# A fused attention and feed-forward kernel: the hand-written order of four engines is rearranged in small steps

## The chip, the cores and the metric

The kernel runs on one core of one Trainium2 chip. A core has a matrix engine (TensorE, PE in the profile; PEld is its weight load, which overlaps the products), three engines for elementwise work (VectorE is DVE, ScalarE is ACT, GpSimd is POOL), and a queue engine (SyncE, SP) that only issues transfers. POOL issues transfers too. The metric is the device time of the whole kernel in microseconds (us). Times inside a trace count from the first instruction of the profiled execution.

## The reference

Four batches of eight heads attend over 768 tokens of 64 features. The tokens are cut into 8 blocks of 96. A small network of weights, 8 by 8 for each batch and head, is made nearly doubly stochastic in five rounds, and k and v are mixed across blocks with it. Attention then runs inside each block. The result, 3072 tokens by 512 features, goes through a feed-forward layer with a leaky rectifier:

```
for _ in range(5):
    P = exp(P - max(P, -1)); P = P / (sum(P, -1) + 1e-9); P = P / (sum(P, -2) + 1e-9)
k_sorted = einsum('bhij,bhjcd->bhicd', P, k_b)       # the same for v
scores = (q_b @ k_sorted^T) / sqrt(64)
attn   = softmax(scores);  x = attn @ v_sorted
h = x @ w_in;  g = max(h, 0) + alpha * min(h, 0);  out = g @ w_out
```

w_in is 512 by 2048, w_out is 2048 by 512.

## The kernel before, in words

The program is a graph of 1190 operations, each with an engine or a choice of engines, its reads and its writes. The list `SEQ` at the head of the file fixes the rest by hand: operations are numbered in the order in which they are added, and an engine runs its operations in the order in which `SEQ` names them. A letter behind a number picks the engine where there is a choice (a for ACT, d for DVE, p for POOL; without one the first of the operation's choices). An entry such as `i6Y` is no operation of the graph: it puts six filler products (128x512, on the identity matrix, their result never read) on PE, into the PSUM bank called Y. `arrange` walks the list; `emit` derives the semaphore waits from reads and writes. So each engine is a queue in order: an instruction that waits holds all that stand behind it on its engine.

The work has these stages. A *group* is one block of one batch, 32 in all; groups 0 to 7 are batch 0.

* **The start.** POOL issues the loads of q, k and v of batch 0 (tiles hT, KS0, VST0), then pieces of v of batch 1 (VST1), the four pieces of w_in, k of batch 1 (KS1), half of w_out, and q of batch 1 (QN). DVE and ACT make P doubly stochastic on 32 partitions. PE runs 208 tiny products (L941), fillers (L1047), and the transposes of q of batch 0 in four pieces (L643); ACT empties those into QTz0. P is spread into the mixing matrix BDK (PE L569, DVE L573).
* **k and v of batch 0.** PE mixes k in six units (L630); ACT and DVE empty each into KT0 (L401, "CAST KT" and "ACTIVATE KT"), and a last small copy KT<-KT fills a gap. For v, eight units: a rearranging copy hT<-VST (ACT, DVE or POOL), a mix on PE (L714), a cast into VS0. Most copies go through one helper and so share line L401; their tiles tell them apart.
* **Attention of batch 0**, by group: scores (L759), the negated maximum nm (DVE L765), scores again in the other orientation with the maximum subtracted (L781, L771), exponent into ET (ACT L804), the product with v (L813, psO or psYP), the reciprocal rec (DVE L821), the scale into xq (DVE L826 as one instruction, or ACT L832 as eight), a transpose on PE (L848) and a copy into xT.
* **k and v of batches 1 to 3.** POOL spreads k and v into tiles with zeros (KSz, L655; VDz, L401), PE mixes them (L668 for k, L709 for v), ACT and DVE cast into KT and VS. Batch 1 needs KS1, which POOL's ninth transfer brings. Attention of groups 8 to 31 uses L756 for scores, nf for the maximum, Esb for the exponent, and transposes by DMA, which SP issues (ET<-Esb, xT<-xq, QTz<-QN).
* **Feed-forward.** The first layer (L875, FFN1) works on chunks of 192 tokens (groups 0 and 1, then 2 and 3), then of 384 tokens, into the two banks of psH; ACT takes the negative part (t<-psH, L885) and DVE combines (hT<-t, L889). The second layer (L915, FFN2) runs for each 128 tokens in four quarters of four products into psYP, later also psS; a copy takes it to outstg, and SP stores it.

PE's products for later stages and for the feed-forward are interleaved in one list, so that PE has work while the other engines prepare the next stage.

Of the kernel before, what the change touches and what calls it, by code (L numbers as in the profile page):

```python
# [33 lines left out]
57 i4H 26 58 29 127 59 60 61 62 21 63 126 64 41 65 66 22 85 67 128 68 87 69 83 88 70 13 71 i6Y 72 86 73 74 75  # L34
129 16 76 77 78 134 79 81 80 130 34 82 96 89 12 38 91 90d 94 95 97d 144 92 98 140 100 84 i9Y 20 101 136 103a
102d 104 17 99d 107a 110 93d 106 105d 111 145 112 108a 146 114 109 154 115 113d 147 15 155 116 148 137 120
117d 118 156 139 119 121d 122 35 157 19 132 124 123d 135 i3Y 125 27 133 158 149 159 i4G 150 160d 151 179 161
180 i2H 152 162d 153 181 36 163 182 188 164 165 166 196 189 205 190 197 192 206 183 191 193 198 207 194 209
184 195 199 185d 213 210 208 186 211 214 221 212 233 187 217 222 138 244 218 215 30 216 200 245 167p 223 201
219 232 202d 248 224 230 246 203 220 142 204 247 266 249 267 258 231 237 234 250 259 251 268 235 141 260 168  # L40
225 269 262 131 261 226 238 227d 263 252 236 239 264 241 286 315d 289 276 228 265 242 305 243 240 253 306 229
280 290 270 279 277 271 293 291 278 272d 287 307 294 292 173 275 295 273 308 170 274d 285 281 297 288 282d 314
296 342 174 283 343 309 284 301 298 310 175 316 311d 302 344 317 299 300 312 345 303 320 313d 328 326 304 321
323d 346 329 332 32 347 169p 348d 324 333 254 353 319 330 331 349 334 255 171p 350 367 335 325 318 382 256 392
383 322 351 393 395 384 394 336 31 352d 365 337 366 357 396 385 416 327 397 398 417 419 399 257 338 176 420
418 400 421 355 422 356d 425 358d 423 339 426 424 428 401 340 427 359 446 354 360d 449 429 447 361 450 368
362d 430 408 451 369 448 409 363 455 364d 431 411 458 456 452 459 410 177 386 453 370 387 457 460 439 388d 371
454 389 479 390d 372 461 402 414 403 488 443 415 404d 476 178 489 480 405 412 477 440 512 406 481 490 438 478
432 485 441d 413 482 433 434d 486 469 513 491 483 487 435 442 484 444 436 509 445d 472 462 510 524 463 506
464d 378 511 470 507 465 377 514 471 466d 508 374 521 525 518 380 522 492 523 519 515 375 526 493 520 379 545  # L50
516d 474 381 542 475 527 560 376 546 554 561 543 468 341 555 544 562 547 473 500 548 501d 499 551 494d 563 502
552 498 556 503d 549 553 535 589 557 550 534 391 590 504 577 505 558d 437 580 578 495 579 581 538 625 591 571
407 496d 582 572 583 533 537 528 586 529 584 530d 536 539 626 585 587 540 569 588 592 531 541 622 532 570d 575
631 623 573 624 627 600 574 172 632 576 598 634 599 601 564 635 602 608 565 628 633 603 610 636 637 609 629
566d 497 606 604 638 655 605d 607 517 639 567 640 373 568d 649 641 611 593 650 652 612 594 595d 656 653 651
642 596 657 597d 654 613 661 643 664 662 667 663 665 658 559 666 684 668 659 676 687 685 696 686 688 677 669
689 697 711 682 690 680 670 702 691 678 693 703 698 467 694 679 683d 704 644 695 699 810 645 692 712 722 646d
660 700 705 713 681 731 714 719 732 723 817 717 720 751 724 744 733 721 728 812 671 725 715 672 729 673d 734
766 718 745 730 752 726 767 647 816 742 706 753 727 618 768 707 674 708d 757 716 743d 748 740 758 754 749 759
741 801 750 755 746 630 621 802 763 747 769 735 619 764 760 736 737d 709 789 776 761 765 803 762 790 813 738  # L60
775 783 777 811 784 786 778d 615 836 785 787 791 620 788 779 792 614 780d 837 617 795 793 781 616 796 770 782d
830 838 797 814 798 846 815d 818 799 839 844 800 831 845 804 819 821 820 864 822 771 848 865 772 832 874 849d
847 824 823 875 833 825 710 850 826 827 834d 851 872 648 828 805 852 873 829 883 853 675 866 854 876 855 877d
701 858 806 807d 856 878 867 884 859 879 860 885 773 857 840 898 841 880 835 899 861 774 881 944 882 862 900
863 892 842d 889 868 893 886 890 808 894 945 869 891 870 887d 756 924 895 925 901 912 896 926 897 888 913 871
906 843 909 950 910 902 951 739 907 946 903 914 908 952 927 911 918 904d 921 794 919 915 953 922 920 923 970
809 932 971 935 933 916d 947 936 934 972 937 981 938 928 973 939 941 940 996 942 982 905 943 958 997 961 959
929 948d 983 962 960 998 963 984 930d 964 985 967 999 1022 968 954 1023 965 1042 955 1010 969 1024 956d 1043
966 957 974 987 975 976d 931 978 988 1011 989 979 986 980 1048 949 993 1049 977 990 994 1012 995 991 917 992
1025 1007 1004 1008 1044 1009 1005 1050 1006 1019 1016 1000 1020 1013 1051 1001 1017 1021 1068 1018 1045 1002d  # L70
1033 1014d 1046 1003 1030 1069 1034 1026 1031 1079 1027 1035 1070 1032 1080 1028d 1039 1071 1036 1040 1081
1041 1037 1029 1038 1052 1059 1053 1054d 1082 1060 1055 1061 1056 1083d 1100 1057 1084 1058 1065 1047 1062
1066 1124 1067 1063 1064 1085 1072 1086 1076 1087 1125 1077 1073 1074 1078 1091 1088 1101 1092 1075 1089 1093
1126 1090 1015 1097 1094 1098 1102 1099 1095 1096 1109 1106 1110 1127 1111 1107 1108 1115 1112 1116 1103 1117
1113 1114 1121 1104d 1118 1122 1166 1119 1120 1172 1123 1130 1133 1131 1145 1134 1135 1146 1132 1139 1136 1140
1184 1141 1137 1167 1138 1151 1142 1152 1147 1153 1143 1144 1173 1128d 1157 1129 1154 1105 1158 1148 1159 1155
1156 1163 1149 1168 1150 1164 1165 1160 1185 1161 1174 1162 1186 1169 1187 1170 1175 1188 1189 1178 1171 1176
1179 1177 1180 1181 1182 1183
# [1011 lines left out]
```

## Time and profile before

| | us |
|---|---|
| median of 3 runs | 234.44 (234.3 to 235.16) |
| the profiled execution's own time | 234.22 |
| its span, first to last instruction | 232.5 |
| PE busy | 221.9 (95% of the span) |
| DVE busy | 166.5 (72%) |
| ACT busy | 157.6 (68%) |
| POOL busy | 102.7 (44%) |
| granted TensorE clock | 1.000 |

A row of the timeline gives start, duration, engine, line, operation, tiles and shapes, how many instructions are merged in the row, and in brackets the idle time before it with what ended it. The duration of a merged row reaches to the modelled end of its last instruction; PE's products are pipelined, so the next row may start before that end. In the chain of waits a row gives start, duration and what the time went to. In the table by stretches, each row gives the stretch, its length, the busy time with the count of instructions, the granted clock, the share of the DMA engines and the rate in GB/s.

### The profile page before, as it was taken

The page shows a single profiled execution, that of the slowest core. Times are in us where ns is not written, and L with a number is a line of the kernel's source. Part 1 is how long each engine was busy: PE and PEld are TensorE (multiplying, and loading weights), DVE is VectorE, ACT ScalarE, POOL GpSimd, SP SyncE. Part 2 cuts the span into 40 slices and gives each one's busy share as a digit, 9 for nine tenths or more (in the row PEclk, how much of TensorE's full clock was granted, in tenths as well). Part 3 has the DMA queues.
Part 4 walks back from the last instruction along what each step waited for, and adds up shares of the span by engine and source line. Part 5 has one row for each costly group of instructions (what it writes and reads, how often), then busy time and mean ns, then how long its engine had stood idle before and what let it go on. Part 6 is the DMA issues. An engine that isn't in the chain of part 4 may idle for free.

```text
span 232.5 us, 6278 instructions
## 1 busy us (share of the span) xinstructions
PE 221.9 (95%) x2516; PEld 139.3 (60%) x2543; DVE 166.5 (72%) x342; ACT 157.6 (68%) x435; POOL 102.7 (44%) x149
## 2 busy tenths in 40 slices
PE   3998999999999999999999999999999999999995
PEld 3456588685666656665665666555555555555553
DVE  5659599896898978696688677758677675463540
ACT  4369667889989596757888587686684764642332
POOL 7999239859076995863999932000000000000000
PEclk9999999999999999999999999999999999999999
DMA  5999999996996699999749998678515533200033
GB/s 70 218 209 197 215 205 186 184 192 116 192 183 124 64 123 170 172 193 206 155 104 137 107 110 181 131 178 171 97 34 143 116 57 121 63 0 0 10 128 135
DMA packets 73389, 31.36 MB, mean 135 GB/s; under 512 B 64512, under 2 KB 68368, under 8 KB 73360
## 3 DMA queue, kind: packets, MB, share of 16 engines
q0 software_dynamic: 24816, 13.63, 43.3%
q1 hardware_dynamic: 48544, 17.33, 37.1%
q8 instruction: 20, 0.33, 0.6%
q14 instruction: 9, 0.07, 0.1%
HBM read 27.28 MB, written 6.29 MB: 144 GB/s over the span
## 4 chain that ended last, share of the span: by engine, by line
PE 76%; POOL 11%; DMA 9%; issue 2%; ACT 0%; POOLq 0%
PE psH L875 32%; PE psYP L915 29%; DMA KS<-in_k_dram 9%; PE psS L915 4%; PE psS L756 3%; POOL KSz L655 3%; PE psO L813 3%; PE psYP L709 2%; PE psYP L668 2%; POOL VDz L401 1%; POOL QN L491 1%; POOL w_in_bf L960 1%; PE psO L915 1%; POOL QN L431 1%; PE psO L848 1%
## 5 line engine op out<-in xcount | busy, mean ns | idle before, releaser
L889 DVE SCALAR_TENSOR_TENSOR hT<-t,omaT,psH 128x384 bf16<-128x384 f32 (+1 forms) x140 | 76.7, 565 | 30.2 <-ACT t L885 29.4
L875 PE MATMUL psH<-xT,w_in_bf 128*128 128x384 bf16 (+1 forms) x560 | 96.9, 310 | 0.3 <-DVE hT L889 0.3
L885 ACT ACTIVATE t<-psH 128x384 f32<-128x384 f32 x126 | 60.6, 494 | 42.9 <-PE psH L875 42.3
L915 PE MATMUL psYP<-w_out_bf,hT 128*128 128x512 bf16 x309 | 78.4, 379 | 1.4
L875 PEld LDWEIGHTS psH<-xT,w_in_bf 128*128 128x128 bf16 x560 | 50.1, 98 | 29.2 <-DVE hT L889 2.7
L793 ACT ACTIVATE Esb<-psS,nf 96x96 bf16<-96x96 f32 x192 | 46.2, 344 | 2.1 <-DVE nf L765 2.0
L915 PEld LDWEIGHTS psYP<-w_out_bf,hT 128*128 128x128 bf16 x336 | 30.5, 98 | 28.1
L401 POOL COPY VDz<-VST 64x384 bf16<-64x384 bf16 x40 | 33.9, 848 | 16.4 <-PE psH L875 6.5
L655 POOL COPY KSz<-KS 64x512 bf16<-64x512 bf16 x36 | 22.1, 613 | 16.5 <-DMA KS<-in_k_dram 8.0
L765 DVE TENSOR_REDUCE nf<-psS 96x8 f32<-96x768 f32 x24 | 22.8, 950 | 8.9 <-PE psS L756 8.6
L431 POOL DMA_DIRECT2D QN<-in_q_dram x24 | 19.9, 846 | 0.7 <-POOL QN L491 0.6
L826 DVE TENSOR_TENSOR xq<-psO,rec 96x512 bf16<-96x512 f32 x27 | 18.4, 683 | 0.5
L813 PEld LDWEIGHTS psO<-VS,ET 112*128 112x128 bf16 x248 | 11.1, 98 | 3.4 <-ACT xT L401 0.5
L813 PE MATMUL psO<-VS,ET 112*128 112x65 bf16 x248 | 12.7, 194 | 0.0
L756 PEld LDWEIGHTS psS<-KT,QTz 128*128 128x128 bf16 (+1 forms) x192 | 10.7, 101 | 3.3 <-ACT Esb L793 0.2
L756 PE MATMUL psS<-KT,QTz 128*128 128x96 bf16 (+1 forms) x192 | 12.2, 206 | 0.0
L401 DVE CAST VS<-psYP 112x512 bf16<-112x512 f32 x15 | 10.3, 689 | 2.3 <-PE psYP L709 2.3
L821 DVE RECIPROCAL rec<-psO 96x8 f32<-96x8 f32 x31 | 6.2, 200 | 6.1 <-PE psO L813 5.7
L709 PEld LDWEIGHTS psYP<-BDV,VDz 128*128 128x128 bf16 x192 | 8.3, 98 | 3.3 <-POOL VDz L401 0.4
L401 ACT ACTIVATE outstg<-psYP 128x512 f32<-128x512 f32 x11 | 6.6, 603 | 5.0 <-PE psYP L915 4.9
L915 PE MATMUL psS<-w_out_bf,hT 128*128 128x512 bf16 (+1 forms) x48 | 9.8, 344 | 0.0
L709 PE MATMUL psYP<-BDV,VDz 128*128 128x64 bf16 x192 | 9.5, 193 | 0.1
(139 smaller groups left out, 209.6 us busy)
## 6 DMA issues: line engine op xcount, KB each, us to landing
out_dram<-outstg SPq DMA_DIRECT2D x23, 256.0 KB, 2.6
KS<-in_k_dram POOLq DMA_DIRECT2D x3, 768.0 KB, 9.1
QN<-in_q_dram POOLq DMA_DIRECT2D x24, 96.0 KB, 3.8
w_in_bf<-in_moe_w_in_dram POOLq DMA_DIRECT2D x4, 512.0 KB, 16.7
w_out_bf<-in_moe_w_out_dram POOLq DMA_DIRECT2D x2, 1024.0 KB, 18.5
VST<-in_v_dram POOLq DMA_DIRECT2D x4, 384.0 KB, 10.1
hT<-in_q_dram POOLq DMA_DIRECT2D x1, 768.0 KB, 7.3
VST<-in_v_dram POOLq DMA_DIRECT2D x1, 768.0 KB, 13.1
```

Source lines behind the costliest of these rows:

```text
L401: return e.activation(o, i, ACTF.Copy) if e is nc.scalar else e.tensor_copy(o, i)
L431: G.add(POOL, lambda e, h=h: e.dma_start(AP(QN, h * 128 + (h // 4) * 64, [[6144, 128], [1024, 6], [1, 64]]), AP(q.tensor, b * HB + h * S * ...
L655: G.add(POOL, lambda e, hp=hp: e.tensor_copy(AP(KSz, hp * 64 * 3072 + u % 3 * 1024 + hp * 64, [[3072, 64], [128, 8], [1, 64]]), AP(KS[n], ...
L709: inst = e.matmul(AP(t, off + dd * 64, [[row, 128], [1, 64]]), AP(VDz, (u % VSL * 8 + dd) * 128, [[VSL * 1024, 128], [1, 128]]), AP(BDV, b ...
L756: inst = e.matmul(o, AP(QTz[n], hp * 3072 + h4 * 768 + i * 96, [[6144, 128], [1, w]]), AP(KT[n], (h4 * 8 + i) * bk, [[ld, 128], [64, 2], [ ...
L765: G.add(DVE, lambda e: e.tensor_reduce(AP(nx, 0, [[8, 96], [4, 2], [1, 4]]), AP(psX, 0, [[1024, 96], [512, 2], [96, 4], [1, 96]]), AxisLis ...
L793: inst = e.activation(AP(Esb[me], p * 128, [[1024, 96], [64, 2], [1, 48]]), AP(psX, (p // 4) * 512 + (p % 4) * 96, [[1024, 96], [48, 2], [ ...
L813: inst = e.matmul(AP(psZ, hp * 512 + h4 * 68, [[1024, 128], [1, 65]]), AP(ET[me] if far else ET[m], pos(h4, hp) * 96, [[800, nk], [1, 128] ...
L875: inst = e.matmul(AP(pt, poff + x * n, [[1024, 128], [1, n]]), AP(w_in_bf, kt * DFF + (ft + x) * 128, [[KT_TILES * DFF, 128], [1, 128]]), ...
L885: G.add(ACT, lambda e: e.activation(AP(t1[tb], 0, [[384, 128], [1, k * n]]), AP(pt, poff, [[1024, 128], [1, k * n]]), ACTF.Relu, scale=-1. ...
L889: G.add(DVE, lambda e, x=x: e.scalar_tensor_tensor(out=AP(hT, (ft + x) * RING + tok % RING, [[FT_TILES * RING, 128], [1, n]]), in0=AP(t1[t ...
L915: inst = e.matmul(AP(bank[0], bank[1], [[1024, 128], [1, n]]), AP(hT, ft * RING + tok % RING, [[FT_TILES * RING, 128], [1, 128]]), AP(w_ou ...
```

## The change

Only the list `SEQ` is different. All operations of the graph are the same, with the same reads and writes; 50 of them run on the other of ACT and DVE; the fillers are 18 in five places instead of 29 in seven. Its first line and the corresponding one of the change:

```
-0 18 1 4 2 7 3 8 42 43 25 10 44 5 33 40 45 46 24 11 37 47 6 48 49 14 50 51 39 52 28 53 9 54 23 55 i1P 143 56
+0 2 11 18 10 3 1 4 17 7 8 42 43 39 25 5 44 9 45 40 24 46 i2G 47 6 48 49 14 i4P 50 33 51 52 53 23 54 143 55 56
```

What this moves is seen on the engines. POOL's order is the same in both, row for row. The order of the other four differs from the start to the end, in most places by a few rows. Three places:

**DVE, from the mixing matrix of batch 0 to the maximum of group 0** (KT0: mixed k of batch 0; hT<-VST0: rearranging copies of v; nm0: the maximum of group 0). Before:

```order
L573 TENSOR_TENSOR BDK<-mkh,psYP 128x128
L509 TENSOR_REDUCE mkjV<-identf 128x8
L401 CAST KT0<-psH 128x32x2x8
L401 CAST KT0<-psO 128x32x2x8
L401 COPY hT<-VST0 128x8x48
L489 MEMSET ET1 128x16
L401 CAST KT0<-psYP 128x32x2x8
L401 COPY KT0<-KT0 128x32x16
L401 COPY hT<-VST0 128x8x48
L765 TENSOR_REDUCE nm0<-psS 96x8
```

and with the change:

```order
L573 TENSOR_TENSOR BDK<-mkh,psYP 128x128
L401 CAST KT0<-psH 128x32x2x8
L537 TENSOR_REDUCE mkhM<-mkh 128x8
L401 CAST KT0<-psO 128x32x2x8
L401 COPY hT<-VST0 128x8x48 x2
L765 TENSOR_REDUCE nm0<-psS 96x8
```

The third cast of k and the copy KT0<-KT0 have left DVE; they stand on ACT now, ahead of ACT's first copy of v. ACT's five casts and copies of k stand around its copy of q's last piece, two before it and three behind it (two and one before the change). On PE the last piece of q is transposed right behind the other three now, ahead of the spread of P, with no fillers between.

**DVE, from the first reciprocals to the spread of the later batches** (rec1, xq1: group 1; rec0, xq0: group 0; nm0: here the maximum of group 2). Before:

```order
L821 RECIPROCAL rec1<-psYP 96x8
L821 RECIPROCAL rec0<-psO 96x8
L826 TENSOR_TENSOR xq1<-psYP,rec1 96x512
L765 TENSOR_REDUCE nm0<-psS 96x8
L401 COPY xT<-psYP 128x4x96
L595 TENSOR_TENSOR outstg3<-psYP,mkj 128x192
```

and with the change:

```order
L821 RECIPROCAL rec1<-psYP 96x8
L821 RECIPROCAL rec0<-psO 96x8
L826 TENSOR_TENSOR xq1<-psYP,rec1 96x512
L826 TENSOR_TENSOR xq0<-psO,rec0 96x512
L765 TENSOR_REDUCE nm0<-psS 96x8
L401 COPY xT<-psO 128x4x96
L595 TENSOR_TENSOR outstg3<-psYP,mkj 128x192
```

The scale of group 0, eight instructions of ACT before, is one of DVE, ahead of group 2's maximum; the copies into xT of groups 0 and 1 have changed places between ACT and DVE.

**PE, around the fourth to sixth unit of k of batch 1** (L668; the rows run from the fourth to the sixth). Before:

```order
L668 MATMUL psYP<-BDM,KSz 128x64 x8
L875 MATMUL psH<-xT,w_in_bf 128x192 x8
L781 MATMUL psS<-QTz0,KT0 128x96 x8
L771 MATMUL psS<-identb,nm0 128x96 x8
L848 MATMUL psO<-identb,xq2 128x96 x4
L668 MATMUL psYP<-BDM,KSz 128x64 x8
L875 MATMUL psH<-xT,w_in_bf 128x192 x8
L759 MATMUL psS<-KT0,QTz0 128x96 x6
L759 MATMUL psS<-KT0,QTz0 96x96 x2
L668 MATMUL psYP<-BDM,KSz 128x64 x8
```

and with the change:

```order
L668 MATMUL psYP<-BDM,KSz 128x64 x8
L781 MATMUL psS<-QTz0,KT0 128x96 x8
L771 MATMUL psS<-identb,nm0 128x96 x8
L875 MATMUL psH<-xT,w_in_bf 128x192 x8
L848 MATMUL psO<-identb,xq2 128x96 x4
L668 MATMUL psYP<-BDM,KSz 128x64 x8
L875 MATMUL psH<-xT,w_in_bf 128x192 x8
L759 MATMUL psS<-KT0,QTz0 128x96 x6
L759 MATMUL psS<-KT0,QTz0 96x96 x2
L668 MATMUL psYP<-BDM,KSz 128x64 x8
```

The second half of a group's scores has moved ahead of a unit of FFN1. From the list's start to the fifth unit of k, PE has the same products in both lists, apart from the fillers, only in another order.

More of the change, by code (lines that the diff above doesn't have):

```diff
@@ L38 @@
[L38 to L62, printed above, removed]
@@ L79 @@
+1181 1182 1183
 """.split()
```

64 lines of the change are left out of this document (44 added, 20 removed).

## The prediction

> **What bounds the kernel now.** I read the table by stretches first, then the chain of waits, then POOL's and PE's timelines. The stretches are cut where FFN1 begins (28.36) and where PE leaves its one longer wait of the middle (46.13):
>
> ```profile
> 0.00:28.36 28.36, 22.64 (x624) 1.00 0.99 181
> 28.36:46.13 17.77, 17.03 (x286) 1.00 1.52 192
> 46.13:229.80 183.67, 182.18 (x1614) 1.00 0.72 122
> ```
>
> From 46.13 on PE is idle for 183.67 - 182.18 = 1.49 us in 184, so PE bounds that part, and no order of the same products can win more than 1.49 there. Ahead of it the chain of waits runs through something else:
>
> ```profile
> 11.76 21.10 DMA KS<-in_k_dram
> 32.92 0.61 POOL KSz L655
> ...
> 45.46 0.62 POOL KSz L655
> 46.53 0.66 PE psH L875 x8
> ```
>
> The transfer of batch 1's k is issued at 11.76 and lands at 32.9; POOL then spreads it, and hands over to PE at 46.1. On the two engines this reads:
>
> ```profile
> 32.92 0.61 POOL L655 COPY KSz<-KS 64x512 bf16<-64x512 bf16 x1 [8.04 <-DMA KS<-in_k_dram]
> ...
> 40.20 4.30 POOL L655 COPY KSz<-KS 64x512 bf16<-64x512 bf16 x6
> 44.56 0.84 POOL L401 COPY VDz<-VST 64x384 bf16<-64x384 bf16 x1
> 45.46 0.61 POOL L655 COPY KSz<-KS 64x512 bf16<-64x512 bf16 x1
> ```
>
> ```profile
> 28.36 0.83 PE L875 MATMUL psH<-xT,w_in_bf 128*128 128x192 bf16 x8
> ...
> 38.30 0.40 PE L668 MATMUL psYP<-BDM,KSz 128*128 128x64 bf16 x8
> ...
> 46.13 0.41 PE L668 MATMUL psYP<-BDM,KSz 128*128 128x64 bf16 x8 [0.36 <-POOL KSz L655]
> ```
>
> POOL sat idle for 8.04 us until the transfer landed, then worked with hardly a gap; its last copy of k ends at 45.46 + 0.61 = 46.07, and the fifth k unit of PE starts at 46.13, after 0.36 us of waiting. So the whole front of the program, 46 us long, is timed by a transfer and POOL, with PE just 0.36 ahead. Whatever is won before this gate is won only if the gate moves.
>
> **The change, part by part.** *The gate.* POOL's list is the same in both programs, row for row, so POOL issues the same nine transfers in the same order. Up to 17.24 it waits for nothing that the change moves: the identity's memset on DVE comes later by the other memsets ahead of it, but POOL reaches it only after 1.31 + 1.02 = 2.33:
>
> ```profile
> 1.31 1.02 POOL hT L426
> ```
>
> ```profile
> DMA  5999999996996699999749998678515533200033
> ```
>
> The page's 40 slices are 5.8 us each; the DMA engines are 90% busy or more from the second to the ninth, so the landing at 32.9 is a matter of bytes, and neither their number nor their order changes. After it POOL waits for two things from elsewhere, the sums that give BDM and freed KSz slots; both came in time before and come no later now. I take the gate at 46.1; an error of 0.3 either way would be one of the transfer rate.
>
> *Fillers.* 29 become 18. In the dense run of nine one filler took 2.12 / 9 = 0.235, so eleven are 2.6 us of PE's time:
>
> ```profile
> 6.46 1.91 PE L1047 MATMUL psH<-identb 128*128 128x512 bf16 x4
> 8.66 1.49 PE L643 MATMUL psO<-identb,hT 128*64 128x128 bf16 x24 [0.29 <-DMA hT<-in_q_dram]
> 15.28 2.12 PE L1047 MATMUL psYP<-identb 128*128 128x512 bf16 x9
> ```
>
> They stand where PE would wait anyway; whether they shorten the front depends on what ends the waits. I look for that now.
>
> *k and v of batch 0.* v lands at 17.24, and ACT is full from there to the product with v:
>
> ```profile
> 17.24 1.62 ACT L401 ACTIVATE hT<-VST 128x384 bf16<-128x384 bf16 x2 [0.29 <-DMA VST<-in_v_dram]
> 18.76 0.69 ACT L401 ACTIVATE VS<-psO 112x512 bf16<-112x512 f32 x1
> 19.31 0.86 ACT L401 ACTIVATE hT<-VST 128x384 bf16<-128x384 bf16 x1
> ...
> 22.52 0.81 ACT L804 ACTIVATE ET<-psH 112x768 bf16<-112x768 f32 x1
> 23.43 0.68 ACT L401 ACTIVATE VS<-psO 112x512 bf16<-112x512 f32 x1
> ```
>
> Three copies of v (0.81 each), four casts (0.69) and two exponents (0.81) are 6.8 us, and 17.24 + 6.8 = 24.05; PE's first product with v began at 24.26. The change gives ACT the same nine operations, and one 0.2 mask besides that stood later. What left DVE is a cast (0.67) and the KT copy (0.34), both ahead of the scores of group 0:
>
> ```profile
> 17.70 0.67 DVE L401 CAST KT<-psYP 128x512 bf16<-128x512 f32 x1
> 18.29 0.34 DVE L401 COPY KT<-KT 128x512 bf16<-128x512 bf16 x1
> 18.69 0.34 PE L759 MATMUL psS<-KT,QTz 64*128 64x96 bf16 x8 [0.43 <-DVE KT L401]
> 24.26 0.41 PE L813 MATMUL psYP<-VS,ET 112*128 112x65 bf16 x8
> ```
>
> The scores can start some 1.0 earlier, but ACT's work behind v's landing hides it. If ACT were not the limit, 1.0 would be won: the bounds are 0 and 1.0 earlier, and I take 0, since the row at 23.43 follows the others without a gap. If ACT's two extra operations on k made it late for v, up to 0.6 (the length of one cast on ACT) would be lost.
>
> *Group 0's outputs.* Here 1.72 on ACT become one instruction of DVE, 0.68 long by the page's row for L826:
>
> ```profile
> 25.08 0.63 DVE L826 TENSOR_TENSOR xq<-psYP,rec 96x512 bf16<-96x512 f32 x1
> 25.19 1.72 ACT L832 ACTIVATE xq<-psO,rec 96x64 bf16<-96x64 f32 x8 [1.07 <-DVE rec L821]
> 26.16 0.95 DVE L765 TENSOR_REDUCE nm<-psS 96x8 bf16<-96x768 f32 x1 [0.45 <-PE psS L759]
> 27.34 0.49 ACT L401 ACTIVATE xT<-psO 128x384 bf16<-128x384 bf16 x1 [0.44 <-PE psO L848]
> ```
>
> DVE would do xq1 to 25.7 and xq0 to 26.4, where ACT ended at 26.91. But the maximum of group 2 stands behind it on DVE and ends at 27.3 instead of 27.11, and group 0's copy into xT stands behind that. I take FFN1's start 0.3 earlier, at about 28.05. The bounds are 0 and the 26.91 - 26.4 = 0.5 that the scale itself gains.
>
> *Sum.* PE comes to the fifth k unit at 46.13 - 0.36 - 0.3 = 45.5, and waits 0.6 there until 46.1. If all eleven fillers and the full 1.0 came off the front, it would arrive at 45.77 - 2.6 - 1.0 = 42.2 and wait 3.9: the product starts at 46.1 all the same. If the front were 0.6 later, PE would arrive at 46.4, 0.3 late. Behind the gate stand the same products as before. I give them the same 183.7, for the ideal was short by 1.49 at most, and the spacings that could cost are nearly those of before: a bank of psH is written again after the other unit and a quarter of FFN2, as before. The tail has the same last four products, copy and store, 232.5 - 229.8 = 2.7, and 234.22 - 232.5 = 1.72 lie around the span. So 46.13 + 183.67 + 2.70 + 1.72 = 234.22 again; the profiled execution was 0.22 below the median of 234.44, inside the runs' spread. I forecast 234.3.
>
> **The rivals.** *A new wait behind the gate (slower).* PE has 1.49 of slack in 184, so any wait there adds in full. The closest place I find: the products with v of groups 22 and 23 had a score, four units of FFN1 and a quarter of FFN2 between them; now one unit (0.65) and one quarter (0.86), 1.5 us. In that time DVE must take the reciprocal and the scale, or psO is not free.
>
> ```profile
> 146.31 0.41 PE L813 MATMUL psO<-VS,ET 112*128 112x65 bf16 x8
> 146.76 0.20 DVE L821 RECIPROCAL rec<-psO 96x8 f32<-96x8 f32 x1 [0.37 <-PE psO L813]
> 149.46 0.68 DVE L826 TENSOR_TENSOR xq<-psO,rec 96x512 bf16<-96x512 f32 x1
> 150.36 0.41 PE L813 MATMUL psO<-VS,ET 112*128 112x65 bf16 x8
> ```
>
> Before, the scale ended at 149.46 + 0.68 = 150.14, 3.6 after the product's 0.24 of issue; with that lag PE would wait 3.6 - 1.5 = 2.1, and the time would be 236.4. Against it: the change lists reciprocal and scale next to each other, 0.45 + 0.2 + 0.7 = 1.35, under 1.5. It decides if DVE is over 0.15 behind; one combine (0.6) ahead would cost half a microsecond, and it takes three such places to leave the band of "same".
>
> *PE at half pace (slower).* The two rows of fillers above show PE at 1.91 / 4 = 0.48 a filler at 6.5 and 0.235 at 15.3, although the granted clock reads 1.00 in both. With fewer fillers PE may come into FFN1 at the slow pace. The 3.4 us from 28.4 to 31.8 would then take 6.8; of the 3.4 lost, 0.3 + 0.36 lie in front of the gate's slack, so 2.7 would show: 237.0. Against it: six fillers, the transposes of q from 8.66 on and the six k units still stand before 17, and from 17 to 28 PE keeps all its products.
>
> [...]
>
> *The gate moves (faster).* If KS landed earlier, or POOL's copies ran quicker, PE could use what the front wins. With the front as I work it out this is 0.36 + 0.3 = 0.7, 233.6, still the same by measure. Only with the fillers' 2.6 in full and a gate 2.6 earlier would it be 234.3 - 3.0 = 231.3. Nothing in POOL's list speaks for it.
>
> *The change does nothing but trade fillers for waits* is what I forecast for the front.
>
> **How the numbers follow.** Same by the gate: 0.75, at 234.3, with its own range 233.6 to 235.2 (0.7 faster by the front and a gate that yields; 0.9 slower by an ACT delay of 0.3 and a 0.6 wait). A new wait behind the gate of over 1.2: 0.11, at 236.4. Half pace: 0.06, at 237.0. A gate that moves: 0.08, at 231.3 to 233.2. What a measurement of this kernel can tell is about 0.5%, 1.2 us. So faster 0.08, same 0.75, slower 0.17. For a range that holds 8 in 10, I go from 233.3 to 235.8: 1.0 below, and 1.5 above for waits that stay smaller than the rival's.
>
> **What would show it.** In the profile after: KS lands at 32.9 and POOL's last copy of k ends near 46.1; the fifth L668 group on PE starts at 46.1 with a wait for KSz of 0.4 to 3; FFN1 starts between 27.5 and 28.4; the stretch from 46.1 to the last product is 183.2 to 185 us long. I am wrong if the fifth L668 group starts before 45.5 (the gate moved), after 46.5 (the front got longer, or PE is slow: then fillers at 15 us take over 0.4), or if the stretch behind it is off by more than 1.2.

## The result and the profile after

| | before | after |
|---|---|---|
| median of the runs shown (4 each) | 234.39 (234.3 to 235.16) | 237.68 (237.22 to 239.24) |
| ratio | 1 | 1.0139 (95%: 1.0106 to 1.0172) |
| profiled execution, span | 234.22, 232.5 | 237.34, 235.6 |
| mean granted clock of the profiled execution | 1.000 | 0.985 |

Medians in this document are over all executions of a kernel; the ratios with their intervals leave out single slow executions, so they need not be the quotients of the medians.

The change makes the kernel 1.4% slower, 3.3 us, where I had forecast no difference. The profiled executions differ by 3.12. Cut at the same three events as in the prediction (FFN1's start, the fifth L668 group, the end of the last product), the table by stretches of the changed kernel reads (the five busy times are those of PE, PEld, DVE, ACT and POOL):

```profile
0.00:31.11 31.11, 21.61 (x612) 14.50 (x613) 19.52 (x65) 16.50 (x31) 22.39 (x36) 0.89 1.00 184
31.11:48.38 17.27, 17.12 (x283) 14.28 (x282) 16.44 (x41) 12.08 (x23) 12.75 (x20) 1.00 1.59 191
48.38:232.94 184.56, 182.65 (x1617) 110.34 (x1641) 132.95 (x240) 123.66 (x359) 67.67 (x94) 1.00 0.70 119
```

FFN1 starts 2.75 later (31.11 against 28.36), the fifth unit 2.25 later (48.38 against 46.13), and the stretch behind it is 0.89 longer (184.56 against 183.67): 2.25 + 0.89 = 3.14. So the loss has two parts, and the larger one lies in the front that I had called free. The first row also has a granted clock of 0.89. Cut finer, the clock is either full or half, in pieces of 3.41 us:

```profile
10.25:13.67 3.42, 1.06 (x52) 1.00 1.01 210
13.67:17.08 3.41, 3.31 (x68) 0.50 1.03 212
17.08:20.50 3.42, 2.85 (x84) 1.00 1.09 197
20.50:23.91 3.41, 1.49 (x60) 1.00 1.12 212
23.91:27.32 3.41, 3.41 (x45) 0.50 1.15 218
```

(stretch, length, PE busy with its products, granted clock, DMA share, GB/s). Each half-clock piece follows one in which PE was idle for most of the time.

A granted clock of 1.00 at the very start is no reading. The trace's clock records begin at 6.84 in the changed kernel and at 11.87 in the kernel before; ahead of its first record the table prints 1.00 for want of one. A filler took 1.91 / 4 = 0.48 there in both kernels (from 4.64 in the changed one, from 6.46 before), against 0.235 later: PE ran at half pace there, and in the kernel before for longer: the first 24 transposes of q took 1.49 there at 8.66, and 0.86 here at 8.63.

PE's timeline shows the idle times:

```profile
8.63 0.86 PE L643 MATMUL psO<-identb,hT 128*64 128x128 bf16 x24 [2.07 <-DMA hT<-in_q_dram]
...
12.22 0.37 PE L569 MATMUL psYP<-Pb,sel 32*128 32x8 bf16 x8 [2.06 <-DVE Pb L562]
...
15.52 2.00 PE L1047 MATMUL psYP<-identb 128*128 128x512 bf16 x5
...
20.77 0.36 PE L714 MATMUL psYP<-BDK,hT 128*64 128x64 bf16 x11
23.05 0.28 PE L714 MATMUL psYP<-BDK,hT 128*64 128x64 bf16 x5 [1.92 <-issue]
...
25.73 1.80 PE L1047 MATMUL psYP<-identb 128*128 128x512 bf16 x4
27.38 0.41 PE L813 MATMUL psYP<-VS,ET 112*128 112x65 bf16 x8
```

Two things are new. Ahead of the spread (L569), where six fillers stood before, PE idles for 2.06. And in the middle of one v unit, between its 11th and 12th product, PE stands still for 1.92 with "issue" as releaser: nothing that the profile shows was awaited. I call this wait the *stall*. At 20.77 PE was 0.32 ahead of the kernel before (the same unit there: 21.09, all 16 products in 0.42); the first product with v comes 3.12 later than there (27.38 against 24.26).

The gate (in the prediction: POOL's copy of k, which held the fifth unit) has changed sides. POOL's copy for the fifth unit now ends at 47.91, since POOL waits for PE on the way, and PE's fifth unit no longer waits for POOL:

```profile
32.51 0.61 POOL L655 COPY KSz<-KS 64x512 bf16<-64x512 bf16 x1 [8.01 <-DMA KS<-in_k_dram]
...
43.32 3.03 POOL L655 COPY KSz<-KS 64x512 bf16<-64x512 bf16 x4 [1.00 <-PE psYP L668]
...
47.30 0.61 POOL L655 COPY KSz<-KS 64x512 bf16<-64x512 bf16 x1
```

### The profile page after: what moved, and what is told of

Read it like the earlier page. It is cut to its first block, busy times and chain, and to the rows that moved or that the text cites. A ratio compares the mean times of both kernels' runs of the same rounds, so it can differ in the third digit from the quotient of the medians.

```text
span 235.6 us, 6222 instructions
## 1 busy us (share of the span) xinstructions
PE 221.4 (94%) x2504; PEld 139.1 (59%) x2532; DVE 168.9 (72%) x344; ACT 152.6 (65%) x412; POOL 102.8 (44%) x149
## 4 chain that ended last, share of the span: by engine, by line
PE 79%; DVE 9%; DMA 5%; ACT 2%; issue 2%; POOL 1%; POOLq 0%
PE psH L875 31%; PE psYP L915 28%; DMA VST<-in_v_dram 5%; DVE hT L889 4%; PE psS L915 4%; PE psS L756 3%; PE psO L813 3%; PE psYP L709 2%; DVE nm L765 1%; PE psYP L668 1%; DVE xq L826 1%; PE psO L714 1%; ACT t L885 1%; PE psO L915 1%; PE psYP L1047 1%
## 5 line engine op out<-in xcount | busy, mean ns | idle before, releaser
L885 ACT ACTIVATE t<-psH 128x384 f32<-128x384 f32 x126 | 61.3, 494 | 47.2 <-PE psH L875 46.3
L915 PE MATMUL psYP<-w_out_bf,hT 128*128 128x512 bf16 x309 | 79.4, 379 | 1.4
L655 POOL COPY KSz<-KS 64x512 bf16<-64x512 bf16 x36 | 22.3, 621 | 18.1 <-PE psYP L668 8.3
L826 DVE TENSOR_TENSOR xq<-psO,rec 96x512 bf16<-96x512 f32 x30 | 20.6, 687 | 0.4
L401 ACT ACTIVATE outstg<-psYP 128x512 f32<-128x512 f32 x14 | 8.4, 599 | 6.8 <-PE psYP L915 6.7
L401 DVE CAST VS<-psYP 112x512 bf16<-112x512 f32 x14 | 9.6, 686 | 1.6 <-PE psYP L709 1.6
L401 ACT ACTIVATE VS<-psYP 112x512 bf16<-112x512 f32 x12 | 8.3, 693 | 3.3 <-PE psYP L714 1.9
L401 ACT ACTIVATE KT<-psYP 128x512 bf16<-128x512 f32 x14 | 8.4, 598 | 2.4 <-PE psYP L668 2.3
## 6 DMA issues: line engine op xcount, KB each, us to landing
w_out_bf<-in_moe_w_out_dram POOLq DMA_DIRECT2D x2, 1024.0 KB, 18.6
```

The lines of the kernel that those rows point to most:

```text
L401: return e.activation(o, i, ACTF.Copy) if e is nc.scalar else e.tensor_copy(o, i)
L655: G.add(POOL, lambda e, hp=hp: e.tensor_copy(AP(KSz, hp * 64 * 3072 + u % 3 * 1024 + hp * 64, [[3072, 64], [128, 8], [1, 64]]), AP(KS[n], ...
L826: return e.tensor_tensor(out=AP(xq[me], 0, [[512, 96], [256, 2], [64, 4], [1, 64]]), in0=AP(psZ, 0, [[1024, 96], [512, 2], [68, 4], [1, 64]]),
L885: G.add(ACT, lambda e: e.activation(AP(t1[tb], 0, [[384, 128], [1, k * n]]), AP(pt, poff, [[1024, 128], [1, k * n]]), ACTF.Relu, scale=-1. ...
L915: inst = e.matmul(AP(bank[0], bank[1], [[1024, 128], [1, n]]), AP(hT, ft * RING + tok % RING, [[FT_TILES * RING, 128], [1, 128]]), AP(w_ou ...
```

## The experiments

Theories at the outset: **clock** (idle from removed fillers brings the half clock), **stall** (the 1.92 by itself, and what follows it), and **order** (the new lists of ACT and DVE). The mean granted clock of an execution counts the half-clock pieces: one is 0.5 x 3.41 / 235 = 0.007, so 0.993 is one, 0.985 two (half pace ahead of the first record is not in it).

### Fillers put back, fillers taken out, one edit alone

The changed kernel with the six fillers back:

```diff
-83 13 70 71 72 88 73
+83 13 70 71 i6Y 72 88 73
```

> The changed kernel with one token put back: the six filler products between q's transposes and the spread of the sort net's weights (24 fillers in all). Clock theory (TensorE falls to half its clock for about 3.4 us after the idle 10.16 to 12.22): that idle is filled, the spread starts at about 12.7, the granted clock stays 1.00 between 13.7 and 17.1, and the five fillers at 15.5 take 1.1 us instead of 2.00; the products ahead of the v units come about 1.3 us earlier than in the changed kernel. Stall theory (the 1.92 us without a releaser in the v unit, and the half clock behind it, are what costs): if the stall does not hang on the clock it stays, with the first product with v at about 26 and a time near 236.5; if it came from the lost clock it goes too, the first product with v is at 24.1 to 24.6 and the time 234.2 to 234.8. Theory that the new order on ScalarE and VectorE is to blame: the time stays at 237.2 to 238.2.

The kernel before without them:

```diff
-70 13 71 i6Y 72 86 73
+70 13 71 72 86 73
```

> The kernel before with one token taken out: the six filler products between q's transposes and the spread (23 fillers are left). Clock theory: TensorE idles for about 2 us ahead of the spread at 12.2 to 12.7, a stretch of about 3.4 us at half clock follows, the nine fillers at 15.3 take up to 3.9 us instead of 2.12, the first product with v is 0.7 to 1.5 us later than 24.26, and the time is 235.0 to 236.0. Theory of the prediction (fillers stand in waits): 234.1 to 234.6, no change. Stall theory: a wait of 1.5 to 2.5 us without a releaser shows up between 20 and 24, and the time is 236 to 238.

The changed kernel with all 29 fillers:

```diff
-i2G ... i4P ... 71 72 ... i5Y ... i4Y ... i3G ... 180 152 162
+i1P ... i4H ... 71 i6Y 72 ... i9Y ... i3Y ... i4G ... 180 i2H 152 162
```

> The changed kernel with the kernel before's 29 fillers at their places (1, 4, 6, 9, 3, 4, 2); the orders of the other engines stay the changed ones. Clock theory and stall theory together (all of the loss came with the fillers): granted clock 1.00 from 12 us on, no wait of over 1 us without a releaser, first product with v at 24.0 to 24.6, time 234.0 to 234.9. Theory that the new order on ScalarE and VectorE is to blame: the time stays over 236.5.

The kernel before with the second edit of the change alone:

```diff
-160d 151 179 161 180 i2H 152 162d 153 181 36 163
+160d 151d 179 161 180 i2H 152 162 153d 163 181 36
```

> The kernel before with the second edit alone: group 0's two outputs scaled by VectorE, the transposed copies exchanged as in the change, all 29 fillers left. Clock and stall theories: nothing of either shows, FFN1 starts 0 to 0.5 us earlier than 28.36, and the last copy of batch 1's k on GpSimd at 46.07 still sets the start of the fifth k unit, so the time is 234.0 to 234.8. Theory that this edit is to blame: 235.5 or more, FFN1 later than 29.

| kernel | median (executions) | ratio to before, 95% | stall in the profile |
|---|---|---|---|
| after_six_back | 237.45 (4; lowest 235.78) | 1.0136 (1.0066 to 1.0206) | none |
| before_six_out | 235.32 (10) | 1.0009 (0.9975 to 1.0043) | none |
| after_29 | 236.52 (10) | 1.0066 (1.0035 to 1.0098) | 2.42 |
| before_scale | 234.38 (10) | 0.9979 (0.9958 to 1.0000) | none |

The kernel before had a median of 234.94 beside these runs (25 executions, 234.22 to 237.77). One execution of each kernel was profiled. That of after_six_back, at 235.78, had no stall; its other three took 237.3 to 240.1, so the six fillers do not bring the old time back. Without the six fillers the kernel before gets the half clock that the clock theory says, and loses nothing clear of the noise by it. In the table of stretches and in PE's timeline:

```profile
9.34:12.75 3.41, 1.23 (x40) 1.00 1.02 212
12.75:16.16 3.41, 3.41 (x109) 0.50 1.06 218
```

```profile
12.38 0.37 PE L569 MATMUL psYP<-Pb,sel 32*128 32x8 bf16 x8 [2.18 <-DVE Pb L562]
...
24.41 0.41 PE L813 MATMUL psYP<-VS,ET 112*128 112x65 bf16 x8
...
46.24 0.41 PE L668 MATMUL psYP<-BDM,KSz 128*128 128x64 bf16 x8 [0.31 <-POOL KSz L655]
```

An idle 2.18, a piece at half clock, and yet the first product with v is just 0.15 later and the fifth unit still waits for POOL. So the removed fillers and the half clock that follows them at 13 are not the loss; there my step on the fillers holds. The clock theory alone falls. The scale on VectorE costs nothing either. FFN1 starts at 28.43 there, but in that execution the first product with v came at 24.70, 0.44 later than before; from that product to FFN1 it takes 3.73 instead of 4.10.

With all 29 fillers back, and the clock full from 11.75 to 25.41, the profiled execution has the stall again (the list is a line shorter in this file, so L714 is L713):

```profile
21.16 0.20 PE L713 MATMUL psYP<-BDK,hT 128*64 128x64 bf16 x2
23.77 0.41 PE L713 MATMUL psYP<-BDK,hT 128*64 128x64 bf16 x14 [2.42 <-issue]
```

In the changed kernel 11 products of that unit ran ahead of the stall, here 2: nine fewer, where nine more fillers stand ahead of it (20 against 11). The stall keeps to a number of products, not to a product: by the trace's records, 478 products stand ahead of it in both. The profiled execution was one of the two slowest of ten (238.5); eight have a granted clock of 1.00 and took 235.3 to 237.1, and whether those stalled is not known. Even so the ratio's interval lies above 1, so the changed order costs something with all fillers in place.

### What happens at a fixed count

Instructions reach the engines by transfers of their own. The page's list of queues has them, alike in both kernels:

```profile
q8 instruction: 20, 0.33, 0.6%
q14 instruction: 9, 0.07, 0.1%
```

0.33 MB in 20 packets is 16 KB a packet, for 2543 products (the kernel before, by its count of weight loads): 127 products a packet. I call what one packet brings a block. I take q8 for TensorE's blocks, since its packets fit TensorE's count, and q14 for other engines'; which ones, the trace doesn't say. The planner in the kernel's own file has a term for such blocks too (`fetched`); I had not used it. So four runs on the count, the first of them the changed kernel once more. That TensorE asks for a block near the 352nd product, and that one loader serves the engines in turn, is theory in these expectations: no trace shows a request.

> The changed kernel once more, unedited, to see whether what its first profile showed comes back. If the stall and the two stretches of half clock belong to the list: again about 2 us without a releaser near the 478th product of TensorE, granted clock 0.985 in most executions, time 237.2 to 238.2. If they are chance: granted clock 1.00 in most executions and a time near 235.5.

> The changed kernel with 144 tiny products in the opening burst instead of 208, so that every later product of TensorE has a number lower by 64. Instruction theory (the stall is TensorE running out of loaded instructions, at a fixed count): no stall in the v unit where the changed kernel had it (its 478th product); a stall, if there is one, again stands at a count near 352, 478 or 606, which is now 64 products further down the list. Theory of an unseen wait of that unit: the stall stays in the same v unit, at about 21. Time: 235.3 to 236.5 if no stall comes, 237 to 238.5 if one comes elsewhere.

> The changed kernel with 240 tiny products in the opening burst instead of 208; every later product of TensorE has a number higher by 32, so that TensorE asks for its next block of instructions some 0.8 us earlier (352 products issued at 14.1 instead of 15.0). Loader theory (one loader fetches instruction blocks for the engines one after the other; in the changed kernel another engine asks just ahead of TensorE at about 15, and TensorE's block comes 2.5 us late): TensorE's block is fetched first, at about 17.5, the other engine's behind it; no wait without a releaser of over 0.5 us near the 478th product; the granted clock is 1.00 or 0.993, and the times lie together at 235.0 to 236.2. Rival (the late block is chance, or belongs to the half clock): the times fall into two heaps as in the changed kernel, half of them at 237 to 238.5.

> The kernel before with 160 tiny products in the opening burst instead of 208; every later product of TensorE has a number lower by 48, so that it has issued 352 at about 18.7 instead of 14.7, later than the other engine's request (about 18.1 there). Loader theory: the other engine's block is fetched first, at about 21, TensorE's only at 23 to 24.5; its 478th product (issued at 22.4 in the kernel before's order) waits 1.5 to 4 us without a releaser, a stretch of half clock follows, and the time is 236.3 to 238, with not one line of the order changed. Rival (the changed order or the fillers make the stall): no wait near the 478th product, 234.2 to 234.8.

Each of the last three changes one number, to 144, to 240, and in the kernel before to 160; the first of them:

```diff
-BURST = 208
+BURST = 144
```

| kernel | median (executions) | ratio to before, 95% | stall near the 478th product |
|---|---|---|---|
| after_again | 237.45 (10) | 1.0088 (1.0049 to 1.0127) | 2.31 |
| after_burst_144 | 238.11 (4) | 1.0117 (1.0083 to 1.0152) | 2.37 |
| after_burst_240 | 235.39 (10) | 1.0035 (1.0008 to 1.0061) | none |
| before_burst_160 | 237.95 (4) | 1.0123 (1.0074 to 1.0173) | 2.20 |

The unedited repeat shows the stall in the same unit, and its ten executions lie in two heaps: 235.06 to 236.34 (four, with at most one half-clock piece) and 237.33 to 238.58 (six, five of them with two or three). With 64 products fewer at the start the stall moves 63 products down the list, into another v unit, behind 477 products:

```profile
22.17 0.60 PE L714 MATMUL psO<-BDK,hT 128*64 128x64 bf16 x26
25.15 0.28 PE L714 MATMUL psO<-BDK,hT 128*64 128x64 bf16 x6 [2.37 <-issue]
```

With 48 fewer, the kernel before gets a stall, without one entry of its list changed, and is as slow as the change:

```profile
22.56 0.22 PE L714 MATMUL psO<-BDK,hT 128*64 128x64 bf16 x1
24.98 0.41 PE L714 MATMUL psO<-BDK,hT 128*64 128x64 bf16 x15 [2.20 <-issue]
...
48.08 0.40 PE L668 MATMUL psYP<-BDM,KSz 128*128 128x64 bf16 x8
```

And with 32 more, the changed kernel loses this stall, though it still has its 18 fillers, an idle 1.72 ahead of the spread and a piece at half clock; it reaches the first product with v at 24.04, and the fifth unit waits for POOL again:

```profile
12.21 0.37 PE L569 MATMUL psYP<-Pb,sel 32*128 32x8 bf16 x8 [1.72 <-DVE Pb L562]
...
24.04 0.41 PE L813 MATMUL psYP<-VS,ET 112*128 112x65 bf16 x8
...
46.44 0.41 PE L668 MATMUL psYP<-BDM,KSz 128*128 128x64 bf16 x8 [0.17 <-POOL KSz L655]
```

It has one of its own instead, 255 products or two blocks earlier. The opening burst is now longer than 223 products, and stops behind that number:

```profile
1.01 2.02 PE L941 MATMUL psS<-bz 32*32 32x32 bf16 x223 [1.01 <-DVE bz L935]
5.32 0.30 PE L941 MATMUL psS<-bz 32*32 32x32 bf16 x17 [2.29 <-issue]
```

All four profiles with a burst of 240 have this wait (2.29 to 2.58); there it costs nothing that shows, since PE would wait for q until 8.6. So the stalls stand behind 223, 477 or 478, and (below) 604 products, about 127 or twice 127 apart, wherever the list puts them.

That the stall is TensorE running out of loaded instructions is my reading of this count together with the packets. I set the packet that moved ahead of the 479th product against the 352nd, 126 products or about one packet earlier, as my estimate of the point where it is asked for: with that count moved from 14.7 in the kernel before to 18.9 in before_burst_160, the packet moved from 18.2 to 22.7. When the packets moved, by the trace's records:

| kernel | 352nd product | other engine's packet | TensorE's packet | 478th product due | stall |
|---|---|---|---|---|---|
| before | 14.7 | 21.5 | 18.2 | 21.1 | none |
| before_six_out | 15.6 | 21.7 | 18.5 | 21.2 | none |
| after_six_back | 15.2 | 18.2 | 18.2 | 21.1 | none |
| after_burst_240 | 14.8 | 18.6 | 17.5 | 20.4 | none |
| after | 15.0 | 18.1 | 20.6 | 20.9 | 1.92 |
| after_again | 15.2 | 18.2 | 20.8 | 20.7 | 2.31 |
| after_29 | 15.5 | 18.6 | 21.5 | 21.2 | 2.42 |
| after_burst_144 | 19.3 | 18.2 | 22.9 | 22.6 | 2.37 |
| before_burst_160 | 18.9 | 20.7 | 22.7 | 22.6 | 2.20 |

The list of transfers of the changed kernel has a packet of q14 in its window from 17.5 to 19 and one of q8 from 20 to 21.5; the kernel before has them the other way round (q8 from 17.5 to 19, q14 from 21 to 22). In all five stalls PE goes on 2.3 to 2.5 after its packet moved; in the four rows without one, packet plus 2.4 is 0.3 to 0.5 ahead of the time due, so even there the margin is thin. There are two ways to be late. In the last two rows the packet comes 3.6 and 3.8 after the 352nd product, as in the rows without a stall (2.7 to 3.5), but PE needs the block 3.3 and 3.7 after it, since it has no fillers and waits left between the two counts. In the three kernels with the changed front it comes 5.6 to 6.0 after, and each time the other engine's packet moved 2.5 to 2.8 ahead of it. That the other engine's request delays TensorE's fits these three, and a race of the two would make two heaps (in after_six_back the two packets moved 0.04 apart), but no run here took the other request away by itself, and the executions of the two heaps were not profiled one by one: argued, not shown. My expectation for before_burst_160 had its stall from that queue; by the packet's 3.8 it came from the short distance.

### What is behind the gate

The next five take the order in the front (up to the gate) and behind the gate apart. front_b_body_a has the list before up to entry 281 (the fifth unit) and the changed one behind; three have the changed front and the list before behind it (24 fillers with bursts of 208 and 240, 18 with 240); after_240_six is the changed list with 24 fillers and a burst of 240.

> The order of the kernel before up to the fifth k unit of batch 1 (29 fillers), and the changed order of everything behind it. Theory that the changed order behind the fifth k unit costs by itself: fifth unit at 46.1, last product at 230.4 to 231.0 (229.5 before), time 235.2 to 235.9. Theory that the whole loss lies in the front (fillers, clock, stall): 234.2 to 234.7.

> The changed order with 24 fillers (the six put back) up to the fifth k unit, and the kernel before's order of everything behind it. If the loss behind the fifth unit belongs to the order there: last product at 229.4 to 229.9, time 234.2 to 234.8 in executions without a stall. If it comes from the changed front (buffers left in another order): 235.5 or more even at a granted clock of 1.00.

> The changed kernel with 240 tiny products in the opening burst and the six fillers back between q's transposes and the spread (24 fillers). By the loader theory no stall, by the clock theory no half clock: granted clock 1.00 in nearly all executions, first product with v at about 24.0, the fifth k unit held at 46.1 to 46.3 by the copies on GpSimd, and the time 235.0 to 235.7, which leaves only what the changed order costs behind the fifth unit (0.6 to 1.2). Rival (the front's order itself costs 2 us): 236.5 or more.

> As the kernel with the changed order and 24 fillers up to the fifth k unit and the kernel before's order behind it, with 240 tiny products in the opening burst. If stall, half clock and the order behind the gate are all of the loss: fifth k unit at 46.1 to 46.3, last product at 229.4 to 229.9, time 234.2 to 234.7, the same as the kernel before, though the first product with v comes at 24.0 instead of 24.26: the gate theory of the prediction. If the front's order costs by itself: over 235.5.

> The changed order with its 18 fillers up to the fifth k unit, the kernel before's order behind it, and 240 tiny products in the opening burst, which keeps TensorE's block at the 478th product in time. Account by parts (stall with its half clock, plus the order behind the fifth unit): the fifth unit at 46.2 to 46.5, the stretch behind it 0.4 to 0.7 us shorter than with the changed order, time 234.5 to 235.0, against 235.39 with the changed order behind. If a new late block comes (at the 606th product, as in the kernel with 24 fillers): a second heap of times at 236.5 or more. If the front's order costs by itself: all executions over 235.5.

| kernel | median (10 each) | ratio, 95% | fifth unit | stretch behind it |
|---|---|---|---|---|
| front_b_body_a | 235.15 | 1.0008 (0.9990 to 1.0025) | 46.18 | 184.37 |
| front_a24_body_b | 235.94 | 1.0040 (1.0013 to 1.0068) | 46.77 | 185.16 |
| after_240_six | 235.80 | 1.0050 (1.0010 to 1.0090) | 46.51 | 184.50 |
| front_a24_body_b_240 | 236.78 | 1.0070 (1.0034 to 1.0105) | 49.74 | 184.36 |
| front_a18_body_b_240 | 235.35 | 1.0006 (0.9984 to 1.0029) | 46.78 | 185.11 |

With the front of before, the order behind the gate costs 0.70 in the profile (184.37 against 183.67), though the median lies just 0.30 above the 234.85 of the kernel before beside it, and the ratio's interval holds 1. The first of its waits stands right behind the gate, and before had none there:

```profile
46.18 0.41 PE L668 MATMUL psYP<-BDM,KSz 128*128 128x64 bf16 x8 [0.46 <-POOL KSz L655]
...
47.94 0.41 PE L668 MATMUL psYP<-BDM,KSz 128*128 128x64 bf16 x8 [0.42 <-ACT KT L401]
```

The next is 0.12 at 61.17, ahead of an FFN1 unit. The reverse half of the account did not close: with the order of before behind a changed front the stretch was 184.36 once and 185.1 twice, the latter by single waits that other profiles of that order do not have (0.33 and 0.26 for VDz at 113 and 119; 0.71 for hT at 183.7). That is no shorter than with the changed order, where five profiles show 184.29 to 184.64, 0.6 to 1.0 over before, and three others 185.1 to 186.0. So these runs cannot divide the 0.89 between the order behind the gate and what a changed front leaves behind: that part of the account stays open.

Three of these profiles have no stall near the 478th product, and yet their fifth unit starts at 46.51 to 46.78 with no wait for KSz. In two of them TensorE's granted clock was 0.50 for a while: from 19.53 to 22.95 in after_240_six, from 14.03 to 17.44 and from 27.69 to 31.10 in front_a18_body_b_240 (mean 0.985). front_a24_body_b has a mean of 1.00; what held its front up is not shown. So without the stall, too, a changed front can overrun the gate, by 0.4 to 0.7.

front_a24_body_b_240 missed my expectation by 2 us, and shows the block once more. Its front is fast, so it comes to the *next* block, behind 604 products, 4.6 after the 478th; the packet moves at 24.27, 4.5 after the 478th, and PE waits until 2.5 after that:

```profile
24.19 0.35 PE L813 MATMUL psO<-VS,ET 112*128 112x65 bf16 x6
26.77 0.24 PE L813 MATMUL psO<-VS,ET 112*128 112x65 bf16 x2 [2.23 <-issue]
```

Three executions of after_240_six (237.6 to 238.4, with two half-clock pieces each) may be the same; they were not profiled. front_a18_body_b_240 waits behind 604 products too, but for 0.36. A longer burst only moves the risk.

### The gate itself

> The kernel before with one swap in GpSimd's list: the last copy of batch 1's k that the fifth k unit needs (0.61 us) goes ahead of a copy of v (0.84 us) that stands before it. Gate theory: the copy ends at 45.2 instead of 46.07, the fifth unit starts without a wait at 45.8, 0.36 us earlier, and all behind it comes earlier by that: 0.1 to 0.4 us less than the kernel before, 233.9 to 234.4 where the kernel before has 234.4. Rival (another wait follows at once, for example for the copy of v): the fifth unit earlier, but the end unchanged or later.

```diff
-272d 287 307 294 292 173 275 295
+272d 275 287 307 294 292 173 295
```

> The same swap on GpSimd together with group 0's outputs scaled by VectorE, the one edit of the change that cost nothing alone. Gate theory: the fifth unit starts at 45.6 to 45.9 without a wait, time 233.8 to 234.3, the lowest of all kernels here, though within what one measurement can tell from the kernel before. Rival: no gain over the kernel before.

before_gate: 234.25 (12 executions), before 234.98 beside it (29), ratio 0.9969 (0.9948 to 0.9990). before_gate_scale: 234.12 (12), 0.9967 (0.9944 to 0.9989). On POOL and PE of before_gate:

```profile
40.37 5.22 POOL L655 COPY KSz<-KS 64x512 bf16<-64x512 bf16 x7
45.66 2.64 POOL L401 COPY VDz<-VST 64x384 bf16<-64x384 bf16 x3
```

```profile
45.65 0.41 PE L668 MATMUL psYP<-BDM,KSz 128*128 128x64 bf16 x8
```

The copy of k ends at 45.59 instead of 46.07, the fifth unit starts 0.48 earlier with 0.10 of wait left, too little for the row to show, and the span is 232.2. In before_gate_scale it starts at 45.93, 0.20 earlier. The gate was real. These two are the only kernels here whose interval lies wholly below the kernel before, by 0.3%; that is less than the 0.5% that I set as the bound, and the medians' 0.7 to 0.9 is more than the 0.48 that the gate can give, so the size of the gain is not settled.

## Why the prediction was wrong

* **The gate**: right as a mechanism. KS landed at 32.51 (forecast 32.9). In five profiles where PE came in time (before_six_out, before_scale, front_b_body_a, after_six_back, after_burst_240) the fifth unit started between 46.18 and 46.44 after a wait for KSz, and moving the gate moved the unit. What I said would show me wrong happened: the fifth unit came after 46.5, at 48.38.
* **Fillers "stand where PE would wait anyway"**: right for the six that before_six_out takes out, 0 clear of the noise at the end. What the step left out is that fillers also count as instructions (after_29 stalls nine products earlier in the list) and that they take up time between two counts (from the 352nd product to the 478th, 5.5 to 6.4 us in seven rows of the table of packets, 3.3 and 3.7 in the last two).
* **The sum of the front, the step that failed.** I had PE come to the fifth k unit at 45.5 and wait 0.6 there. That took PE's arrival from engines, buffers and transfers of data, and had no term for instructions; PE came at 48.38 and did not wait. Term by term: without the stall the changed front reaches the first product with v at 24.00 (after_six_back), inside the 23.90 to 24.70 of the profiles with the front of before and no stall, so the 0 that I had taken for k and v of batch 0 stands. In the changed kernel PE was another 0.23 ahead of that at the stalled unit (20.77 against 21.00); then 1.92 of stall, and 3.41 / 2 = 1.70 for the half clock behind it: 24.00 - 0.23 + 1.92 + 1.70 = 27.39, and the row says 27.38 (that it closes to 0.01 is chance, as the start of the sum is another execution). In after_burst_144 and before_burst_160 no half clock follows the stall, and the first product with v comes at 26.40 and 26.71, about 2.4 late: the stall alone. Of the 3.4 that the changed kernel lost up to there (27.38 - 24.00) the slack up to the gate took 1.2 back: the fifth unit is 48.38 - 46.21 = 2.17 behind after_six_back, 2.25 behind the kernel before.
* **PE at half pace**, the rival with chance 0.06: its sign and nearly its time (237.0) came true, by another cause, which is luck. The 3.4 us in its sum is a term that no run shows at FFN1's start; what the runs showed in its place is half clock in pieces of 3.41 us, at 13.67 and 23.91 in the changed kernel. Half clock behind the six removed fillers cost nothing in before_six_out; behind the stall it nearly doubles the price (1.70 on top of 1.92). The 1.00 that I read at 6.5 as the granted clock was no record (they begin at 11.87): PE was at half pace there, with 0.48 a filler. Waits of 1.9 to 2.2, each nearly or wholly inside one piece of 3.41, stood ahead of the half clock (2.06 and 1.92 in the changed kernel, 2.18 in before_six_out).
* **Behind the gate the same 183.7**: 184.56, 0.89 more, inside the 1.2 I allowed. The rival with a price of 2.1 at groups 22 and 23 did not come; no wait is shown there. My reading that PE was idle for 1.49 was wrong: that profile has 1614 products behind the gate but 1640 weight loads, so 26 products are missing from the records. before_six_out has the same order there and all 1640 products: 183.66 long, 183.58 busy, so idle is 0.08. after_again, also complete, has the changed order: 184.64 long, 184.20 busy. In the table by stretches:

```profile
46.24:229.90 183.66, 183.58 (x1640) 110.24 (x1640) 131.28 (x237) 126.62 (x373) 68.03 (x94) 1.00 0.73 122
48.57:233.21 184.64, 184.20 (x1644) 110.29 (x1641) 132.97 (x240) 123.50 (x359) 67.42 (x94) 1.00 0.73 119
```

  Of the 0.98 between these two only 0.36 is waits (the largest 0.24, at 86, for hT); the rest is time in which PE counts as busy with the same products, and no run here explains it.
* **Group 0's outputs**: forecast FFN1 0.3 earlier, and right: from the first product with v to FFN1 it takes 3.73 in before_scale, and 31.11 - 27.38 = 3.73 in the changed kernel, against 28.36 - 24.26 = 4.10 before, 0.37 less. Each is one execution, but three more profiles without the edit (before_six_out, front_b_body_a, before_gate) show 4.09 to 4.11, and before_gate_scale 3.76. The gate and the stall hide the gain.
* **Range and chances**: the range ended at 235.8, since its upper end was made from waits for data alone.

## What to carry to other kernels

This kernel of 2543 products, many of them small, was held up by the delivery of its instructions, 1.92 to 2.42 us a stall near the 478th product: count products per block (127 here), and read whether the time between two counts leaves room for the next block (5.9 us between them in the changed kernel, and its packet moved 5.6 behind the first). Its mark here was a wait with "issue" as releaser in the middle of a unit, which kept to a count (478 products in the changed kernel and in after_29), not to a line. Before calling a change of order free, look at what it does to the spacing of these counts on the densest engine, and run more than one execution, since one list gave two heaps of times here. Six fillers in a wait cost nothing here, but a stall that left 1.49 us of work in one clock piece cost half a piece more. Before reading idle time off a profile, compare its count of products with that of weight loads.

## What the hardware did that I had not expected

* TensorE's packet of instructions moved 2.7 to 3.8 us after the 352nd product, my estimate of the point where it is asked for, in six of the nine profiles in the table, and 5.6 to 6.0 in three; for the next block in front_a24_body_b_240 it moved 4.5 after the 478th. In the five stalls of the table PE went on 2.3 to 2.5 after it moved. These lags lie in a stretch where the DMA engines are 90% busy and more (the second to the eighth of the page's slices, in both kernels).
* In the records the granted clock changes only at the edges of pieces of 3.41 us. Pieces with PE busy 1.06, 1.23 and 1.49 us were followed by half clock. In before_burst_160 a stall of 2.20 fell on the edge of two pieces, each 2.30 busy, and the clock stayed full:

```profile
20.48:23.89 3.41, 2.30 (x79) 1.00 1.12 213
23.89:27.31 3.42, 2.30 (x52) 1.00 1.13 213
```

  So 31 to 44% of a piece ahead of half clock was still work (1.06 of 3.42, 1.49 of 3.41).
* Some pieces do not follow a simple bound on busy time: 6.84 to 10.25 of the changed kernel, with 1.53 us busy, was followed by full clock. In front_a18_body_b_240 a piece with 2.45 busy (24.27 to 27.69) was followed by half clock, and in after_burst_144 one with 1.80 (23.54 to 26.95) by full clock. In front_a24_body_b_240 one with 3.00 busy at half clock (27.71 to 31.12) was followed by half clock again. What sets the clock stays open.
